# The third matrix's chains in a fused Winograd MLP: differences, roundings and products moved against each other

## The chip, the cores and the metric

The kernel runs on one core of a Trainium2 chip. The metric is device time in microseconds (us) of one launch. TensorE (PE in the profile) multiplies, VectorE (DVE) and ScalarE (ACT) work between the products, GpSimd (POOL) takes differences and sums from SBUF, and SyncE (SP) issues nearly all the DMAs. Each engine runs its own instructions strictly in order.

## The reference

For x of 2 x 3008 x 256, two filters of 1505 x 256 and the weights of two MLPs:

```
y  = irfft(rfft(x, axis=1) * (filt_r + 1j*filt_i))      # then 6016 x 256
h  = y @ w_in;  z = (h * sigmoid(h)) @ w_out             # w_in 256 x 2048, w_out 2048 x 256
g  = z @ w_gate; v = z @ w_val                           # 256 x 1536 each
out = (g * sigmoid(g) * v) @ w_out2                      # 1536 x 256
```

All inputs and outputs are float32. TensorE multiplies rounded values (fp32r), so each operand is split into a rounded high part (a cast on ScalarE) and a rest (a subtraction on VectorE), and each product is three matmuls.

## The kernel before, in words

The transform and the first MLP fill the first half. The change lies in the second MLP, which runs from about 585 us to the end.

**Pairs.** The 6016 tokens are cut into six blocks of up to 1024, and the 1536 hidden columns into six parts. `Pair(t, u)` computes one part for one block, 36 pairs in all. Gate and value are each one 2x2 block product in Winograd's form with seven products: numbers 1, 2 and 4 take weights that stay in SBUF (`w`), numbers 3, 5, 6, 7 weights loaded per pair (`wst`, `load_s2`). A `Gate` leaves its results in PSUM banks. Their order in code is `p15`, `p6`, product 2, `p3`, `p7`, `p4`. `p7` ends with an addition on VectorE (line 885) that reads the bank that `p4` then adds to, so the first matmul of `p4` waits for it; ScalarE copies out or moves a bank at lines 852, 855 and 870. For the gate, `p4` comes after the value's `p15`, for the value after the next pair's `p15`. The pair leaves two tiles, `ga` (upper half of the products, pool `late["p"]`) and `c` (pool `mid`), in `raw[u]`.

**Chains.** The third matrix takes two pairs' tiles (p = 0, 1), so there are 18 chains, three per block, of 14 steps each: seven products in the order of `AT7 = (1, 5, 6, 2, 7, 3, 4)`, each for both p. A step's work is spread over time by `tick()`, which each pair calls seven times:

- `product7` (line 1110): three matmuls of step i, put in a queue that PE drains between the pair's matmuls, one for two of those.
- `lower7` (line 1066, VectorE): the rest `ho` of step i + AHEAD - 1.
- `high7` (line 1061, ScalarE): the rounding `ho` of step i + AHEAD, in a new tile of `mid`.
- `sum7` (line 1056, GpSimd): the difference that products 5, 6, 7 and 4 need, of step i + AHEAD + 2. In place in `ga` for 5 and 7 and in `c` for 4, in a tile `x6` for 6. Number 7 overwrites the operand of 1, number 4 that of 2, so each waits until `lower7` has read it.
- `load7` (line 1074, SyncE): the weights `w7` of two products (512 KB), issued eight steps ahead, in a tile of `mid`.

When a product is complete, `after7` copies or adds it (lines 1082 to 1097), and GpSimd adds at line 1104.

**Order.** It is written out by hand: the program order of each engine is that of the code, `clock` says how far the chain is behind the pairs (it starts at -16 and goes up by one per tick), and `later(u, k, ...)` hangs loads, splits of the next block's operands (`xo`, lines 784 and 787), differences (`xr`, line 767) and the output (`store2`, VectorE transposes and DMAs) on the k-th place in pair u. After the last pair the remaining ticks run by themselves.

**Tiles.** `mid` has 33 tiles of 4 KB per partition, one kind for all names (`ho`, `w7`, `wst`, `c`, `x6`, `x2`, `xr`, `xo`, `oa`, `ob` and nine tiles of weights that stay). In the second MLP `late["p"]` is a pool `last` of nine tiles of the same size, which only `ga` uses. A new tile waits for the last reader of the tile whose place it takes.

Of the kernel before, what the change touches and what calls it, by code (L numbers as in the profile page):

```python
# [12 lines left out]
F32R = mybir.dt.float32r  # L13
U32 = mybir.dt.uint32
AF = mybir.ActivationFunctionType
ALU = mybir.AluOpType
# [13 lines left out]
P = 128  # L30
# [89 lines left out]
def fft_filter_mlp_kernel(  # L120
# [13 lines left out]
    nc = tc.nc  # L134
# [47 lines left out]
    def mid(shape, name, dtype=F32):  # L182
        return mp.tile(shape, dtype, tag="mid", name=name)
# [237 lines left out]
    wt, late = {}, {}  # L421
# [328 lines left out]
    def size2(t):  # L750
        return min(STEP2, NTOK - STEP2 * t)
# [204 lines left out]
    class Pair:  # L956
# [27 lines left out]
        def run(self, old, side):  # L984
# [5 lines left out]
            if old:  # L990
                old.tail()
            side(-1)
            tick()
            g.p6()
            if old:
                old.join()
            side(0)
            tick()
            g.add(g.a, 2, last=True)
            a = late["p"].tile([P, STEP2], F32, tag="mid", name="ga")  # L1000
# [3 lines left out]
            g.p3()  # L1004
            nc.scalar.activation(a[:, n:m], g.b, AF.Silu)
            tick()
            g.p7()
            side(1)
# [22 lines left out]
            self.join()  # L1031

    raw, x6, ops7, w7, low7, done7 = {}, {}, {}, {}, {}, {}
    AHEAD = 3
    clock = [-16]

    def where(i):
        c, r = divmod(i, 14)
        return c, AT7[r // 2], r % 2

    def view(c, k, p):
        u = 2 * c + p
        n = size2(u // 6) // 2
        a, b = raw[u]
        if k == 6:
            return x6[c][:, p, :n]
        v, l = {1: (a, 0), 5: (a, 1), 7: (a, 0), 2: (b, 0), 4: (b, 0), 3: (b, 1)}[k]
        return v[:, n * l:n * l + n]

    def sum7(c, k, p):  # L1050

        if k == 6 and p == 0:
            x6[c] = mid([P, 2, 512], "x6")
        if k in (5, 6, 7, 4):
            a, b = {5: (5, 1), 6: (3, 5), 7: (6, 1), 4: (2, 6)}[k]
            nc.gpsimd.tensor_tensor(view(c, k, p), view(c, a, p), view(c, b, p), op=ALU.subtract)  # L1056

    def high7(c, k, p):
        x = ops7[c, k, p] = mid([P, 2, 512], "ho", F32R)
        v = view(c, k, p)  # L1060
        nc.scalar.copy(x[:, 0, :v.shape[-1]], v)  # L1061

    def lower7(c, k, p):
        x, v = ops7[c, k, p], view(c, k, p)
        n = v.shape[-1]
        nc.vector.tensor_tensor(x[:, 1, :n], v, x[:, 0, :n], op=ALU.subtract)  # L1066
        if k == 4:
            del raw[2 * c + p]

    def load7(c, r):  # L1070
        q = c % 3
        w = mid([P, 2, 512], "w7", F32R)
        n = min(2, 7 - 2 * r)
        nc.sync.dma_start(w[:, :n].bitcast(F32), d7[q][:, 2 * r:2 * r + n])
        for i in range(n):
            w7[c, AT7[2 * r + i]] = w[:, i].rearrange("p (j l c) -> p j l c", j=2, l=2)
# [41 lines left out]
    CHAINS = 3 * NBLK2  # L1118

    def tick():  # L1120
        i = clock[0]
        clock[0] += 1
        inside = lambda i: 0 <= i < 14 * CHAINS
        if inside(i):
            queue.extend((product7, *where(i), k) for k in range(3))
        if inside(i + AHEAD - 1):
            lower7(*where(i + AHEAD - 1))
        if inside(i + AHEAD):
            high7(*where(i + AHEAD))
        if inside(i + AHEAD + 2):  # L1130
            sum7(*where(i + AHEAD + 2))
        if inside(i + 8):
            c, r = divmod(i + 8, 14)
            if r % 4 == 0:
                load7(c, r // 4)
# [78 lines left out]
    for b in range(len(WIDE)):  # L1214
        i = len(units) + 32 * b
# [10 lines left out]
    for q in range(4):  # L1226
        i = (22, 42, 60, 67)[q]
# [24 lines left out]
    later = lambda u, k, fn, *args: todo2.setdefault((u, k), []).append((fn, args))  # L1252
# [7 lines left out]
    later(0, 0, split_x2, 0, 4)  # L1260
    for t in range(1, NBLK2):
        for m in range(2):
            later(6 * t + 2 + m, 1, store2, t - 1, m)
        u = 6 * t - 6
        later(u + 2, 0, load_x2, t)
        later(u + 3, 1, prep_x2, t, 0)
        later(u + 3, 3, prep_x2, t, 1)
        for k, n in ((0, 1), (1, 5), (3, 6)):
            later(u + 4, k, split_x2, t, n)

        for k, n in ((3, 2), (4, 3), (4, 7)):
            later(u + 5, k, split_x2, t, n)
        later(u + 6, 0, split_x2, t, 4)
# [6 lines left out]
    for k in range(FILL_X, 8):  # L1280
        i = 8 + 5 * k // 2
# [6 lines left out]
    for h in range(12):  # L1288
        q, i = h // 2, 31 + 5 * h // 2
# [258 lines left out]
```

## Time and profile before

| | us |
|---|---|
| median of three runs | 1222.85 |
| lowest, highest | 1219.66, 1224.13 |
| profiled execution, its own time | 1225.84 |
| its span, first to last instruction | 1224.1 |
| PE busy | 1137.0 |
| DVE busy | 898.8 |
| ACT busy | 787.8 |
| POOL busy | 557.8 |

Busy time is the union of an engine's instructions in the profiled execution. Between the span and the execution's own time lie 1.7 us. In timelines a row gives start, duration, engine, line, operation and tiles; what stands in brackets is how long the engine had been idle before and what ended that.

### The profile page before, as it was taken

The page shows a single profiled execution, that of the slowest core. Times are in us where ns is not written, and L with a number is a line of the kernel's source. Part 1 is how long each engine was busy: PE and PEld are TensorE (multiplying, and loading weights), DVE is VectorE, ACT ScalarE, POOL GpSimd, SP SyncE. Part 2 cuts the span into 40 slices and gives each one's busy share as a digit, 9 for nine tenths or more (in the row PEclk, how much of TensorE's full clock was granted, in tenths as well). Part 3 has the DMA queues.
Part 4 walks back from the last instruction along what each step waited for, and adds up shares of the span by engine and source line. Part 5 has one row for each costly group of instructions (what it writes and reads, how often), then busy time and mean ns, then how long its engine had stood idle before and what let it go on. Part 6 is the DMA issues. An engine that isn't in the chain of part 4 may idle for free.

```text
span 1224.1 us, 15232 instructions
## 1 busy us (share of the span) xinstructions
PE 1137.0 (93%) x4993; PEld 921.4 (75%) x4993; DVE 898.8 (73%) x1262; ACT 787.8 (64%) x1482; POOL 557.8 (46%) x423
## 2 busy tenths in 40 slices
PE   9999999999999999999997898889789879978985
PEld 7588888988888888888775676677567657757873
DVE  5977455665766867866486887779688787958986
ACT  5798666676777776855665566566556655656662
POOL 3658545633424536231063455346354544625444
PEclk9999999999999999999999999999999999999997
DMA  9964442364544554454443353445245334534531
GB/s 253 293 194 122 144 153 87 121 211 146 169 152 156 197 190 155 155 198 154 158 169 103 129 163 122 129 131 163 95 126 161 110 129 145 144 111 135 142 121 30
DMA packets 130110, 182.45 MB, mean 149 GB/s; under 512 B 56816, under 2 KB 84336, under 8 KB 130032
## 3 DMA queue, kind: packets, MB, share of 16 engines
q1 hardware_dynamic: 129584, 181.29, 46.7%
q8 instruction: 39, 0.64, 0.2%
q14 instruction: 39, 0.32, 0.1%
q10 hardware_dynamic: 448, 0.20, 0.1%
HBM read 138.99 MB, written 42.47 MB: 148 GB/s over the span
## 4 chain that ended last, share of the span: by engine, by line
PE 69%; DVE 16%; ACT 5%; issue 5%; DMA 3%; POOL 2%; DVEq 0%; SPq 0%; ACTq 0%; POOLq 0%
PE bk L818 16%; PE acc L731 14%; PE bk L1110 7%; DVE ho L1066 6%; PE acc L708 6%; PE h L658 6%; PE y L818 5%; PE xa L818 4%; PE xb L818 4%; DMA w<-d 2%; PE s L209 2%; DVE c L885 2%; PE s L397 2%; DVE bk L879 2%; PE s L206 1%
## 5 line engine op out<-in xcount | busy, mean ns | idle before, releaser
L818 PE MATMUL bk<-xo,wst 128*128 128x512 f32 (+1 forms) x864 | 290.1, 397 | 21.4 <-ACT u L870 13.2
L1110 PE MATMUL bk<-ho,w 128*128 128x512 f32 (+1 forms) x756 | 288.2, 399 | 3.5 <-DVE ho L1066 3.5
L731 PE MATMUL acc<-h,w 128*128 128x512 f32 x768 | 283.6, 389 | 0.0
L818 PE MATMUL bk<-xo,w 128*128 128x512 f32 (+1 forms) x648 | 218.9, 403 | 48.8 <-DVE c L885 48.5
L818 PEld LDWEIGHTS bk<-xo,wst 128*128 128x128 f32 x864 | 164.3, 192 | 65.3 <-ACT u L870 19.6
L818 PEld LDWEIGHTS bk<-xo,w 128*128 128x128 f32 x648 | 124.3, 194 | 87.9 <-DVE c L885 46.0
L1110 PEld LDWEIGHTS bk<-ho,w 128*128 128x128 f32 x756 | 147.4, 196 | 33.4 <-DVE ho L1066 6.7
L731 PEld LDWEIGHTS acc<-h,w 128*128 128x128 f32 x768 | 144.2, 188 | 29.7
L1066 DVE TENSOR_TENSOR ho<-ga,ho 128x512 fp32r<-128x512 f32 (+1 forms) x108 | 118.0, 1094 | 12.4 <-ACT ho L1061 12.4
L1056 POOL TENSOR_TENSOR c<-c,x 128x512 f32<-128x512 f32 (+1 forms) x36 | 57.5, 1611 | 146.8 <-DVE ho L1066 136.8
L1061 ACT CAST ho<-ga 128x512 fp32r<-128x512 f32 (+1 forms) x108 | 66.2, 613 | 45.8 <-POOL c L1056 28.4
L708 PE MATMUL acc<-h,w 128*128 128x512 f32 (+1 forms) x384 | 95.4, 376 | 0.0
L1104 POOL TENSOR_TENSOR oa<-oa,s 128x512 f32<-128x512 f32 (+1 forms) x24 | 34.8, 1452 | 131.0 <-DVE s L1082 131.0
L1066 DVE TENSOR_TENSOR ho<-c,ho 128x512 fp32r<-128x512 f32 (+1 forms) x108 | 92.5, 876 | 0.0
L1056 POOL TENSOR_TENSOR ga<-ga 128x512 f32<-128x512 f32 (+1 forms) x36 | 57.0, 1586 | 62.3 <-DVE ga L1022 62.3
L658 PE MATMUL h<-xh,w 128*128 128x512 f32 (+1 forms) x248 | 83.6, 379 | 0.1
L708 PEld LDWEIGHTS acc<-h,w 128*128 128x128 f32 x384 | 71.2, 188 | 11.2
L666 DVE TENSOR_TENSOR h<-h,h 128x512 fp32r<-128x512 f32 (+1 forms) x64 | 41.4, 655 | 47.8 <-ACT h L665 46.4
L818 PE MATMUL xa<-xo,w 128*128 128x512 f32 x192 | 75.3, 394 | 0.0
L818 PE MATMUL y<-xo,wst 128*128 128x512 f32 x192 | 74.7, 389 | 0.0
L1061 ACT CAST ho<-c 128x512 fp32r<-128x512 f32 (+1 forms) x108 | 65.3, 614 | 14.3 <-PE bk L818 5.1
L818 PE MATMUL xb<-xo,wst 128*128 128x512 f32 x192 | 74.5, 390 | 0.0
(153 smaller groups left out, 2345.5 us busy)
## 6 DMA issues: line engine op xcount, KB each, us to landing
w<-d SPq DMA_DIRECT2D x54, 512.0 KB, 3.6
wst<-ds_g SPq DMA_DIRECT2D x36, 512.0 KB, 4.1
wst<-ds_v SPq DMA_DIRECT2D x36, 512.0 KB, 3.4
wst<-ds SPq DMA_DIRECT2D x32, 512.0 KB, 4.8
zt<-d SPq DMA_DIRECT2D x16, 384.0 KB, 4.7
d<-z SPq DMA_DIRECT2D x11, 512.0 KB, 4.4
d<-x SPq DMA_DIRECT2D x22, 256.0 KB, 2.3
d<-wst SPq DMA_DIRECT2D x21, 256.0 KB, 2.2
```

The lines of the kernel that those rows point to most:

```text
L209: nc.tensor.matmul(o, csp[:k, mp_, r:r + n], x[xp_], start=(i == 0), stop=(i == 2))
L397: nc.tensor.matmul(ps[:, col:col + n], zt_of[c // 2, g][:, 3 * (c % 2) + t, :], c4[:, o:o + n], start=(t == 0), stop=(t == 2), skip_group_ ...
L658: nc.tensor.matmul(ps[:, :n], wt[key, f // 4, g][:, wpart, o:o + P], x[xpart][:, g, :n], start=(g == 0 and k == 0), stop=(g == 1 and k == 2),)
L666: nc.vector.tensor_tensor(h[:, 1, :n], u[:, :n], h[:, 0, :n], op=ALU.subtract)
L708: nc.tensor.matmul(a[:, :n], w[:, wpart, o:o + 128], h[:, xpart, :n], start=(f == 0 and k == 0), stop=(f == 15 and k == 2),)
L731: nc.tensor.matmul(a, w[:, wpart, o:o + 128], h[xpart][:, n * l:n * l + n], start=(f == 0 and k == 0), stop=(end and k == 1), skip_group_c ...
L818: nc.tensor.matmul(o, w(wpart), x[:, xpart, :o.shape[-1]], start=(first and k == 0), stop=(last and k == 2), skip_group_check=True,)
L1056: nc.gpsimd.tensor_tensor(view(c, k, p), view(c, a, p), view(c, b, p), op=ALU.subtract)
L1061: nc.scalar.copy(x[:, 0, :v.shape[-1]], v)
L1066: nc.vector.tensor_tensor(x[:, 1, :n], v, x[:, 0, :n], op=ALU.subtract)
L1104: nc.gpsimd.tensor_tensor(o, o, s, op=ALU.add)
L1110: nc.tensor.matmul(o, w7[c, k][:, p, wpart], ops7[c, k, p][:, xpart, :n], start=(k in (1, 5) and p == 0 and i == 0), stop=(k in (2, 3, 4) ...
```

## The change

```diff
-    AHEAD = 3
-    clock = [-16]
+    AHEAD = 4
+    clock = [-20]
+    SUMS = {-7: (5, 0), -6: (5, 1), -4: (6, 0), -3: (6, 1), 1: (7, 0), 2: (7, 1), 5: (4, 0), 6: (4, 1)}
...
         if k == 6 and p == 0:
             x6[c] = mid([P, 2, 512], "x6")
-        if k in (5, 6, 7, 4):
-            a, b = {5: (5, 1), 6: (3, 5), 7: (6, 1), 4: (2, 6)}[k]
-            nc.gpsimd.tensor_tensor(view(c, k, p), view(c, a, p), view(c, b, p), op=ALU.subtract)
+        a, b = {5: (5, 1), 6: (3, 5), 7: (6, 1), 4: (2, 6)}[k]
+        nc.gpsimd.tensor_tensor(view(c, k, p), view(c, a, p), view(c, b, p), op=ALU.subtract)
...
-        w = mid([P, 2, 512], "w7", F32R)
+        w = late["p"].tile([P, 2, 512], F32R, tag="mid", name="w7")
...
-        if inside(i + AHEAD + 2):
-            sum7(*where(i + AHEAD + 2))
+        for o in (0, 14):
+            c, r = divmod(i + o, 14)
+            if 0 <= c < CHAINS and r - o in SUMS:
+                sum7(c, *SUMS[r - o])
...
-            later(6 * t + 2 + m, 1, store2, t - 1, m)
+            later(6 * t + 3 + m, 1, store2, t - 1, m)
```

The chain's products come four ticks later against the pairs. Roundings are four steps ahead of their product, rests three. The eight differences of a chain, before at steps -3, -2, -1, 0, 3, 4, 7 and 8 of that chain, are at steps -7, -6, -4, -3, 1, 2, 5 and 6. `w7` takes its tiles from `last`, which `ga` uses, and no longer from `mid`. `store2` is called one pair later.

## Rows read from the trace of the kernel before

**Rows 1.** The waits of PE, 585 to 1213 us: total, times, longest (us).
```profile
PE bk L818 <- DVE c L885: 48.5, 33, 3.4
PE bk L818 <- ACT u L870: 13.2, 15, 1.6
PE bk L818 <- ACT bk L852: 7.8, 8, 1.2
```
**Rows 2.** Busy time by stretch: PE, PEld, DVE, ACT, POOL (instructions), clock, DMA.
```profile
822.84:928.74 105.90, 92.50 (x379) 72.26 (x379) 84.38 (x112) 63.87 (x121) 49.79 (x32) 0.97 0.44 132
865.65:869.05 3.40, 3.40 (x10) 2.63 (x11) 0.00 (x0) 1.72 (x4) 0.00 (x0) 0.57 0.00 0
906.60:910.00 3.40, 3.40 (x10) 2.65 (x9) 1.30 (x2) 2.27 (x5) 0.22 (x1) 0.56 0.29 82
1193.50:1213.00 19.50, 15.37 (x52) 10.98 (x50) 18.82 (x24) 6.70 (x14) 12.19 (x9) 0.84 0.00 0
585.00:1193.50 608.50, 538.34 (x2249) 428.27 (x2248) 477.16 (x638) 371.31 (x709) 274.14 (x179) 0.97 0.44 135
```
**Rows 3.** Timeline of PE: two matmuls of a stretch without gaps.
```profile
917.59 0.39 PE L1110 MATMUL bk<-ho,w 128*128 128x512 f32 x1
...
918.27 0.39 PE L1110 MATMUL bk<-ho,w 128*128 128x512 f32 x1
```
**Rows 4.** Timeline of PE: gaps of the block that begins at 822.84 us.
```profile
822.84 0.96 PE L818 MATMUL bk<-xo,w 128*128 128x512 f32 x3 [0.56 <-DVE c L885]
...
850.29 0.50 PE L818 MATMUL bk<-xo,wst 128*128 128x512 f32 x1 [0.62 <-ACT u L870]
...
865.37 1.22 PE L818 MATMUL bk<-xo,wst 128*128 128x512 f32 x2 [1.25 <-ACT bk L852]
...
876.21 0.98 PE L818 MATMUL bk<-xo,w 128*128 128x512 f32 x3 [2.29 <-DVE c L885]
...
882.17 0.74 PE L818 MATMUL bk<-xo,wst 128*128 128x512 f32 x2 [1.54 <-ACT u L870]
...
904.74 0.47 PE L818 MATMUL bk<-xo,w 128*128 128x512 f32 x1 [3.41 <-DVE c L885]
```
**Rows 5.** Timeline of POOL and ACT and DVE, 859 to 881 us.
```profile
859.76 3.42 POOL L1056 TENSOR_TENSOR ga<-x,ga 128x512 f32<-128x512 f32 x2
...
869.29 0.62 ACT L1061 CAST ho<-x 128x512 fp32r<-128x512 f32 x1 [1.92 <-PE bk L1110]
...
871.68 0.62 ACT L784 CAST xo<-xr 128x512 fp32r<-128x512 f32 x1 [1.28 <-PE bk L818]
...
872.33 0.69 DVE L787 TENSOR_TENSOR xo<-xr,xo 128x512 fp32r<-128x512 f32 x1 [6.77 <-ACT xo L784]
...
877.56 2.93 POOL L1056 TENSOR_TENSOR c<-c,x 128x512 f32<-128x512 f32 x2 [14.39 <-DVE ho L1066]
...
880.52 0.62 ACT L1061 CAST ho<-ga 128x512 fp32r<-128x512 f32 x1 [5.70 <-POOL c L1056]
```
**Rows 6.** Timeline of POOL and DVE, 898 to 919 us.
```profile
898.81 1.74 POOL L1056 TENSOR_TENSOR ga<-ga 128x512 f32<-128x512 f32 x1
899.32 1.77 DVE L1066 TENSOR_TENSOR ho<-ga,ho 128x512 fp32r<-128x512 f32 x1
...
902.22 1.78 DVE L1066 TENSOR_TENSOR ho<-ga,ho 128x512 fp32r<-128x512 f32 x1
...
903.41 3.41 POOL L1056 TENSOR_TENSOR ga<-x,ga 128x512 f32<-128x512 f32 x2
903.92 0.68 DVE L885 TENSOR_TENSOR c<-bk,s 128x512 f32<-128x512 f32 x1
...
918.47 0.68 DVE L1066 TENSOR_TENSOR ho<-ga,ho 128x512 fp32r<-128x512 f32 x1
```
**Rows 7.** The waits of SP's queue, 600 to 1224 us: total, times, longest (us).
```profile
SPq L1074 <- PE bk L1110: 166.2, 39, 9.8
SPq L637 <- PE bk L1110: 108.2, 37, 4.3
```

## The prediction

> **What bounds the kernel now.** I read the waits of PE first, then busy time by stretch, then the gaps of PE one by one in one block of the second MLP, and last what ACT, DVE and POOL did before each gap. Six pairs make a block, and a block repeats. From 822.84 to 928.74 us it takes 105.90 us and PE runs 379 matmuls [rows 2]; by count they are 6 x 63 = 378, a pair's own 42 and 21 of the chains. In a stretch without gaps three matmuls take 918.27 - 917.59 = 0.68 us, 0.227 each [rows 3]. 378 x 0.227 = 85.8 us, so 20.1 us of a block are lost. Eleven gaps of over 0.3 us sum to 13.3. Two stretches of 3.4 us at a granted clock of 0.57 and 0.56 [rows 2], nearly all of them at 1.2 GHz, come right behind gaps (865.37, 904.74 [rows 4]) and cost half their length, 1.7 us each. The other 3.4 us are slower starts behind gaps. The whole stretch of pairs is 608.5 us [rows 2], or 5.75 blocks.
>
> The gaps are of two kinds. Five (0.56, 0.47, 1.09, 1.25, 3.41, sum 6.78; first and last in [rows 4]) are waits for line 885 on a DVE that is late because its subtractions collide with POOL. The rest of a chain's operand (line 1066) takes 0.68 us alone and 1.77 or 1.78 beside a difference on POOL; line 885, which reads PSUM, keeps its 0.68 beside one [rows 6]. I call these collisions. Before the last gap POOL runs (5,1), both 6 and both 7 without a break, 898.81 to 906.82 [rows 6].
>
> The other six (0.62, 0.52, 1.25, 0.33, 2.29, 1.54, sum 6.55; four of them in [rows 4]) begin on ACT. Its cast of x at 869.29 waited 1.92 us for PE line 1110, though the value was ready when POOL began the next difference at 859.76 [rows 5]: what it waited for was a tile of `mid`, held by an earlier matmul. The split at 871.68 waited 1.28 for the same kind of thing, DVE stood 6.77 us behind that split [rows 5], its line 885 came late and PE lost 2.29 [rows 4]. Then ACT's cast of a 7 stood 5.70 us until the second difference of 4 was done, long after its own difference had ended (859.76 + 3.42 = 863.18) [rows 5]: again a tile, and PE lost 1.54. SP says the same of `mid`: loads of `w7` waited 166.2 us for PE, `wst` 108.2 [rows 7]. `mid` is full at nearly every point. So tiles and collisions, not one busy engine, hold PE: 48.5 us show as line 885 and 13.2 + 7.8 as copies of ACT [rows 1].
>
> **The change part by part.** One step of a chain is a tick, 105.90 / 42 = 2.52 us [rows 2].
>
> *w7 out of `mid`.* Three tiles per chain live 12 steps (8 ahead, 4 of products) and the last 10: 46 steps in 14, 3.3 tiles. What the other edits add to `mid`: `ho` one step longer, 14 steps in 14, 1.0; `c` from p = 0 lives 23 steps for 20, from p = 1 17 for 14, 6 in 14, 0.4; `x6` 10 for 9, 0.1. Net 1.8 of 33 tiles become spare. The six gaps above need releases that come 0.3 to 2.3 us earlier. `mid` hands out some 13 tiles per pair of 105.90 / 6 = 17.65 us (seven `ho`, two `c`, two `wst`, a part of the others), so 1.8 tiles are 1.8 x 17.65 / 13 = 2.4 us. I take five of the six as gone and one of 1.25 as left: 5.3 us per block. Bounds: all of 6.55, or nothing if the choice of the free tile still takes a fresh one.
>
> *Differences earlier.* The instructions are the same eight per chain, 24 per block. Before, each cast came two steps after its difference; now there are three to five steps, 7 to 12 us. This removes what true waits of ACT on POOL there are; they are within the six gaps, so it earns nothing twice. On POOL's queue they stand between the additions of line 1104, which wait for products: the order becomes (5,0), (5,1), addition, both 6, addition, both 7, both 4, so no run longer than about three replaces the run of five. Collisions per difference stay as likely as they are; only their bunching falls. DVE has 84.38 busy of 105.90 [rows 2], so a delay of one collision, 1.1 us (1.78 - 0.68 [rows 6]), is mostly absorbed by the 18 matmuls (18 x 0.227 = 4.1 us) between `p7` and `p4`, and three in a row are not. Bounds for the five gaps: all 6.78 stay, or half go; I take a quarter, 1.7, nearer to the row where a single collision costs PE 0.56.
>
> *Clock.* One of the two slow stretches stands behind a gap of ACT (1.25 at 865.37 [rows 4]) that goes, the other behind the collision of 3.41 that only shrinks. One goes: 1.7 us. Bounds none and 3.4.
>
> *Chain later, rests and roundings one step earlier.* ACT and DVE do the same work, PE the same matmuls. The cast of product 1 for p = 1 stood one step behind the tick in which its `ga` is made, now four. What was hidden by pairs and now isn't is the end: 12 matmuls of 448 columns leave the stretch of pairs and run behind the last pair. There DVE is busy 18.82 of 19.50 us, so DVE sets the pace [rows 2]. Three more rests at 0.68 to 1.78 and two more additions at about 0.6 make 3.2 to 6.5 us; the pairs give back 12 x 0.227 = 2.7 at most, and some of the differences finish before that stretch. I put +1 us, between -1 and +4.
>
> *`store2` a pair later.* Same transposes and DMAs; the last ones, which nothing follows, don't move. Its two `oa` are held 40 steps for 37 or as long as before, nothing that matters.
>
> *`w7` in `last`.* `ga` lives 23 and 17 steps, 40 in 14, 2.9 tiles; with 3.3 that is 6.1 of nine, and eight at the peak (step 4: four `ga`, four `w7`). SP's queue has `wst` and `x2` behind each `w7` load; with a spare tile they go earlier, not later. Cost 0 in the forecast; the other end is a rival below.
>
> Sum per block: 5.3 + 1.7 + 1.7 = 8.7 us. I don't take all of it: a faster PE brings DVE from 84.4 / 105.9 = 0.80 to 84.4 / 97.2 = 0.87 busy, in strict order, and new gaps must come. I take a third off, 5.8. Times 5.75 it is 33 us, less 1 at the end: 1225.8 - 32 = 1194 for the profiled execution. The median of before lies 3.0 us under that execution, so 1191.
>
> **The rivals.**
>
> *Only tiles help (A).* Collisions keep their number and move: both 7, which ran in the gate's half of the even pair, now come in its value half, and both 4 in the gate's half of the odd pair. Then 5.3, less a third, is 3.5 per block: 20 us, 1225.8 - 20 + 1 - 3 = 1204. For it: a rest beside POOL takes 1.78 wherever it stands [rows 6]. Against it: four of the five gaps come from runs, not single differences. The Trainium skill (SBUF — State Buffer, "Who interferes with whom") says that a VectorE instruction with two SBUF inputs and a GpSimd one that reads SBUF exclude each other for a whole instruction, the second waiting for the first. By that rule spreading differences lowers no sum of delays, and the time would be the 1204 of this rival; the rows agree on the size of one delay, but don't show what spacing does.
>
> *DVE gives it all back (B).* DVE's 84.4 us per block are already near PE's 85.8, so PE finds it late whatever is freed: 1223. Against it: DVE idles 21.5 us per block, 6.77 of it at one place because of a tile [rows 5].
>
> *Nine tiles are too few (C), slower.* If PE falls over four steps behind the ticks, an old `w7` is still unread when a new `ga` is wanted; nine are live, and ACT's silu, ahead of the copies that PE needs, waits. Price: one such wait of 1.92 (as at 869.29 [rows 5]) per chain, 18 x 1.92 = 35 us, against the 20 of A: 1223 + 15 = 1238. It decides from nine live tiles on; by count there are eight at most, so it needs the lag or an unlucky choice of the place.
>
> **How the numbers follow.** Forecast 0.52, A 0.22, B 0.12, C 0.14. About 0.5% (6 us) is what a measurement tells from no change. Faster by more: forecast 0.52, A 0.20, B 0.02, together 0.74. Within: A 0.02, B 0.08, C 0.01: 0.11. Slower: B 0.02, C 0.13: 0.15. The range: at the low end all of 6.55, 1.7 and 1.7 with nothing given back, 10 per block, 57 us, and a little of the second slow stretch: 1164. At the high end it takes in B and the beginning of C: 1228. Forecast alone: 1175 to 1205.
>
> **What would show it.** Tiles right: SP's 166.2 us for `w7` on PE fall under 60, ACT no longer waits for POOL's differences of 4, DVE's 6.77 us behind the split is gone, and the gaps at copies of ACT (21.0 us in all [rows 1]) fall under 8. Collisions right: waits for line 885 fall from 48.5 to about 25 to 30, none over 2.5 us, while rests beside POOL still take 1.78. Half-speed stretches: one per block. Forecast wrong: `ga`'s silu waiting for a tile, or gaps at line 885 of the old sum at new places, or POOL's run as long as before because the additions don't divide it.

## The result, and the profile after

The changed kernel takes 1182.82 us (median of three runs, 1182.42 to 1185.03), the kernel before 1222.85: a ratio of 0.9676, interval 0.9648 to 0.9703, 40.0 us less. The profiled execution takes 1185.03 us with a span of 1183.2, against 1225.84 and 1224.1.

The first view is busy time by stretch, with the columns of [rows 2]: one block, the half-speed stretch behind its largest gap, and the end behind the last pair.

```profile
819.99:919.06 99.07, 91.07 (x378) 72.03 (x378) 83.58 (x112) 64.01 (x121) 47.43 (x32) 0.97 0.46 141
...
846.25:853.08 6.83, 6.20 (x15) 4.32 (x15) 3.92 (x6) 4.34 (x8) 2.56 (x2) 0.50 0.69 135
...
1149.50:1172.00 22.50, 18.87 (x66) 13.72 (x66) 21.97 (x28) 8.10 (x17) 14.40 (x11) 0.85 0.01 4
```

A block takes 99.07 us for 105.90 with the same 378 matmuls by count. From 585 us on the pairs take 564.5 us for 608.5, 44.0 less: 6.83 us times 5.75 blocks are 39.3 of it, and up to 2.7 are the matmuls of the chains that now run behind the last pair. The end holds 14 more matmuls in these windows (12 by count) and takes 22.5 us for 19.5. So the span is 40.9 us shorter. PE's waits of the second MLP answer to [rows 1]:

```profile
PE bk L818 <- DVE c L885: 31.1, 31, 3.2
PE bk L818 <- ACT bk L852: 5.3, 6, 2.1
PE bk L1110 <- DVE ho L1066: 2.2, 4, 0.6
PE bk L818 <- ACT u L870: 1.8, 2, 1.7
```

Gaps that begin at a copy of ACT fell from 21.0 to 7.1 us in all, those at line 885 from 48.5 to 31.1. In PE's timeline the block shows seven gaps of over 0.2 us for eleven [rows 4]:

```profile
845.27 0.50 PE L818 MATMUL bk<-xo,w 128*128 128x512 f32 x1 [3.21 <-DVE c L885]
847.62 1.22 PE L818 MATMUL bk<-xo,wst 128*128 128x512 f32 x2 [0.64 <-ACT bk L852]
871.23 0.96 PE L818 MATMUL bk<-xo,w 128*128 128x512 f32 x3 [0.25 <-DVE c L885]
880.54 0.47 PE L818 MATMUL bk<-xo,w 128*128 128x512 f32 x1 [1.99 <-DVE c L885]
888.80 0.96 PE L818 MATMUL bk<-xo,w 128*128 128x512 f32 x3 [0.74 <-DVE c L885]
910.77 0.50 PE L818 MATMUL bk<-xo,w 128*128 128x512 f32 x1 [0.36 <-DVE c L885]
919.06 0.98 PE L818 MATMUL bk<-xo,w 128*128 128x512 f32 x3 [0.74 <-DVE c L885]
```

They sum to 7.93 us for 13.33. Of the six gaps that were put down to tiles one is left, 0.64 for 6.55. The gaps at line 885, which the prediction put down to collisions, have not shrunk: 7.29 for 6.78. The largest of them is again a DVE that reaches line 885 late, as in [rows 6], here behind a split (787) and a rest (1066) that both stood beside differences of 6. In this view of ACT, DVE and POOL the split takes 1.82 us and the rest 1.77:

```profile
838.66 0.62 ACT L784 CAST xo<-x 128x512 fp32r<-128x512 f32 x1 [1.20 <-DVE c L982]
839.29 2.98 POOL L1056 TENSOR_TENSOR x<-c,ga 128x512 f32<-128x512 f32 x2 [2.46 <-ACT xo L784]
...
839.31 1.82 DVE L787 TENSOR_TENSOR xo<-x,xo 128x512 fp32r<-128x512 f32 x1 [0.73 <-ACT xo L784]
...
841.05 1.77 DVE L1066 TENSOR_TENSOR ho<-c,ho 128x512 fp32r<-128x512 f32 x1
...
844.54 0.68 DVE L885 TENSOR_TENSOR c<-bk,s 128x512 f32<-128x512 f32 x1
```

Not all of the 3.21 us is collision. The split's cast on ACT stood 1.20 us for line 982, whose result it doesn't read, which is how a wait for a tile looks; DVE idled 0.73 us behind that cast, and POOL's differences of 6, which don't read its result either, were let go by the same cast. By this reading a wait for a tile set the two side by side.

SP's queue answers to [rows 7]: loads of `w7` hardly wait for a tile any more, `wst`, which stayed in the large pool, waits longer.

```profile
SPq L637 <- PE bk L1110: 190.3, 33, 7.9
...
SPq L1074 <- PE bk L1110: 6.1, 1, 6.1
```

### The profile page after: what moved, and what is told of

Read it like the earlier page. It is cut to its first block, busy times and chain, and to the rows that moved or that the text cites. A ratio compares the mean times of both kernels' runs of the same rounds, so it can differ in the third digit from the quotient of the medians.

```text
span 1183.2 us, 15182 instructions
## 1 busy us (share of the span) xinstructions
PE 1127.6 (95%) x4993; PEld 919.2 (78%) x4993; DVE 887.5 (75%) x1262; ACT 788.0 (67%) x1482; POOL 544.9 (46%) x423
## 4 chain that ended last, share of the span: by engine, by line
PE 73%; DVE 17%; issue 4%; ACT 3%; DMA 1%; POOL 0%; DVEq 0%; ACTq 0%; SPq 0%; POOLq 0%
PE bk L818 16%; PE acc L731 15%; PE bk L1110 8%; PE acc L708 7%; PE h L658 7%; DVE ho L1066 6%; PE y L818 6%; PE xa L818 4%; PE xb L818 4%; DVE bk L879 2%; PE s L397 2%; DVE c L885 2%; PE s L209 2%; PE s L206 2%; DVE ga L1019 1%
## 5 line engine op out<-in xcount | busy, mean ns | idle before, releaser
L818 PE MATMUL bk<-xo,wst 128*128 128x512 f32 (+1 forms) x864 | 284.9, 393 | 5.0 <-ACT bk L852 3.1
L818 PE MATMUL bk<-xo,w 128*128 128x512 f32 (+1 forms) x648 | 216.0, 398 | 33.6 <-DVE c L885 31.1
L818 PEld LDWEIGHTS bk<-xo,w 128*128 128x128 f32 x648 | 121.7, 191 | 72.5 <-DVE c L885 37.7
L1066 DVE TENSOR_TENSOR ho<-ga,ho 128x512 fp32r<-128x512 f32 (+1 forms) x108 | 105.6, 980 | 0.6 <-ACT ho L1061 0.6
L1056 POOL TENSOR_TENSOR c<-c,x 128x512 f32<-128x512 f32 (+1 forms) x36 | 52.6, 1463 | 113.9 <-DVE ho L1066 113.9
L1066 DVE TENSOR_TENSOR ho<-c,ho 128x512 fp32r<-128x512 f32 (+1 forms) x108 | 102.3, 953 | 0.2 <-issue 0.2
L1056 POOL TENSOR_TENSOR ga<-ga 128x512 f32<-128x512 f32 (+1 forms) x36 | 47.8, 1331 | 88.4 <-DVE ga L1022 76.7
L708 PEld LDWEIGHTS acc<-h,w 128*128 128x128 f32 x384 | 71.2, 188 | 11.2
L852 ACT COPY bk<-bk 128x512 f32<-128x512 f32 (+1 forms) x72 | 41.3, 573 | 45.1 <-PE bk L818 45.0
L1056 POOL TENSOR_TENSOR ga<-x,ga 128x512 f32<-128x512 f32 (+1 forms) x36 | 50.1, 1407 | 33.5 <-DVE ho L1066 29.7
```

The lines of the kernel that those rows point to most:

```text
L708: nc.tensor.matmul(a[:, :n], w[:, wpart, o:o + 128], h[:, xpart, :n], start=(f == 0 and k == 0), stop=(f == 15 and k == 2),)
L818: nc.tensor.matmul(o, w(wpart), x[:, xpart, :o.shape[-1]], start=(first and k == 0), stop=(last and k == 2), skip_group_check=True,)
L852: nc.scalar.copy(self.y, self.a)
```

## The experiments

All times are medians of three or more runs beside runs of the kernel before on the same chip (medians of before 1221.1 to 1223.8). "Spare" is the count of tiles that the large pool has free against before, by steps held as in the prediction: +3.3 for `w7`, -1.0 for roundings four ahead, -0.4 to -0.6 for the later chain's `c`, -0.1 for a longer `x6`. The later chain always comes with `store2` a pair later. The count is a mean and doesn't rank the kernels: -0.6 takes 1231.10 us and -0.2 takes 1248.80, and the kernel with the most spare tiles is not the fastest.

| kernel | spare | us | ratio to before (interval) |
|---|---|---|---|
| before | 0 | 1222.9 | 1 |
| `w7` alone | +3.3 | 1192.67 | 0.9742 (0.9717 to 0.9767) |
| later chain alone | -0.6 | 1231.10 | 1.0081 (1.0054 to 1.0107) |
| `w7`, later chain | +2.7 | 1169.18 | 0.9563 (0.9532 to 0.9593) |
| the same, 32 tiles | +1.7 | 1179.13 | 0.9655 (0.9632 to 0.9678) |
| `w7`, later, roundings four ahead | +1.9 | 1178.84 | 0.9632 (0.9603 to 0.9661) |
| the same and differences spread: the change | +1.8 | 1182.82 | 0.9676 (0.9648 to 0.9703) |
| the change, 31 tiles | -0.2 | 1248.80 | 1.0207 (1.0181 to 1.0232) |
| the change, roundings three ahead | +2.6 | 1169.50 | 0.9576 (0.9549 to 0.9603) |

**The `w7` alone.**

```diff
-        w = mid([P, 2, 512], "w7", F32R)
+        w = late["p"].tile([P, 2, 512], F32R, tag="mid", name="w7")
```

> The kernel before with one edit: the weights w7 take their tiles from the pool of nine instead of the pool of 33; differences, roundings, products and store2 stand where they were. Theory T (tiles): the gaps of PE that begin on ACT come from tiles of the large pool, and 3.3 tiles become spare, so nearly all of those gaps go: a block takes 100 to 102 us for 105.9, and the whole 1190 to 1203 us; waits for line 885 stay at 45 to 55 us. Rival S (spacing): what helped is that the differences stand earlier and apart; then this kernel gains little, 1212 to 1223 us. Rival C (nine tiles too few): 1225 us or more.

It took 1192.67 us, 31 us less than before, as theory T had it. Its waits of PE:

```profile
PE bk L818 <- DVE c L885: 45.3, 32, 3.4
PE bk L1110 <- DVE ho L1066: 3.1, 6, 0.6
PE bk L818 <- ACT u L870: 1.6, 1, 1.6
```

21.0 us of gaps at copies of ACT [rows 1] are down to 1.6, and line 885 keeps 45.3 of its 48.5. The order of the work was not touched: one pool had too few tiles.

**The change with 31 tiles.**

```diff
-    mp = pool("mp", 33)
+    mp = pool("mp", 31)
```

> The changed kernel with 31 tiles in the large pool for 33, which takes the 1.8 spare tiles by count away again; the order of all instructions is unchanged. Theory T: the gaps that begin on ACT come back, 1205 to 1225 us (a part of it may fall in the first half, to be read by stretch). Rival S: the order sets the time, so 1180 to 1190 us.

It took 1248.80 us, 66 more than the change and beyond the expectation. At most 1.4 us of it lie before the second MLP, whose first copy at line 852 starts at 587.2 us for 585.8. PE's waits, and below them one cast of ACT with the idle time before it:

```profile
PE bk L818 <- ACT bk L852: 44.2, 20, 7.7
PE bk L818 <- DVE c L885: 35.2, 35, 2.3
```

```profile
875.12 0.62 ACT L1061 CAST ho<-ga 128x512 fp32r<-128x512 f32 x1 [4.54 <-DMA out_dram<-ob]
```

Line 885 costs 35.2 us for 31.1 in the change, while 44.2 us for 5.3 now begin at ACT's line 852; with them the granted clock of the pairs falls from 0.98 to 0.95. The cast reads `ga` and writes `ho`; it has nothing to do with the output, and yet it waits 4.54 us for an output DMA. The only tie between them is the tile: `ho` gets the place of an `ob` that is still being stored. That is how such a wait is told from a true one.

**Differences near again.** `SUMS` is no longer used, each difference stands two steps ahead of its rounding (`sum7` gets its test for products 5, 6, 7 and 4 back, not shown):

```diff
-        for o in (0, 14):
-            c, r = divmod(i + o, 14)
-            if 0 <= c < CHAINS and r - o in SUMS:
-                sum7(c, *SUMS[r - o])
+        if inside(i + AHEAD + 2):
+            sum7(*where(i + AHEAD + 2))
```

> The changed kernel with one part undone: each difference stands two steps ahead of its rounding again, in one run of four and two pairs, and no longer three to five steps ahead and spread; the chain is still four steps later, roundings four ahead, w7 in the pool of nine. Theory T: spacing is worth little, 1180 to 1192 us. Rival S: the spread is worth most of the 40 us, so 1205 to 1222 us here.

It took 1178.84 us, 4 us less than with the spread. So in the change the spread earned no time, against the prediction's 1.7 us per block. Rival S falls. PE's waits are nearly the same in all, 39.4 us here at line 885 and copies of ACT (34.4, 3.1 and 1.9) for 38.2 in the change; the granted clock of the pairs is 0.99 for 0.98.

**No differences.** The change without the 144 differences of the chains:

```diff
-            if 0 <= c < CHAINS and r - o in SUMS:
-                sum7(c, *SUMS[r - o])
...
-        if k == 6:
-            return x6[c][:, p, :n]
-        v, l = {1: (a, 0), 5: (a, 1), 7: (a, 0), 2: (b, 0), 4: (b, 0), 3: (b, 1)}[k]
+        v, l = {1: (a, 0), 5: (a, 1), 7: (a, 0), 2: (b, 0), 4: (b, 0), 3: (b, 1), 6: (b, 1)}[k]
```

> The changed kernel without the 144 differences of the chains on GpSimd (products 5, 6, 7 and 4 of the third matrix get operands that lack them, so that part of the output is left out); everything else stands as in the changed kernel. It prices the collisions of VectorE with these differences and any wait for them. Theory T with collisions: the waits for line 885 (31 us) fall under 8, rests at line 1066 take 0.68 us, the half-speed stretches in the pairs go, and the time is 1140 to 1155 us. Rival (VectorE is simply full, collisions are hidden): 1172 to 1183 us.

It took 1138.98 us, just under the expected 1140. PE's first wait, and one of its gaps:

```profile
PE bk L818 <- DVE c L885: 11.2, 15, 1.5
```

```profile
767.83 0.47 PE L818 MATMUL bk<-xo,w 128*128 128x512 f32 x1 [1.40 <-DVE c L885]
```

and the rests (line number 1064 here), in the view by line:

```profile
L1064 DVE TENSOR_TENSOR ho<-c,ho 128x512 fp32r<-128x512 f32 (+1 forms) x144 | 105.9, 741 | 0.3
L1064 DVE TENSOR_TENSOR ho<-ga,ho 128x512 fp32r<-128x512 f32 (+1 forms) x108 | 78.4, 728 | 0.6 <-ACT ho L1059 0.6
```

A rest takes 0.73 to 0.74 us on the mean, and waits at line 885 fall from 31.1 to 11.2, a little above the 8 expected. Without the differences the kernel is 1182.8 - 1139.0 = 44 us faster. That holds collisions and half-speed, but also what else goes with the differences: the casts' waits for them, and the tile of `x6`, which is held 10 of 14 steps and of which this kernel has no need. The run doesn't divide the 44. The gap of 1.40 stands where the change has 1.99 (880.54): so 1.4 of that one is a full DVE queue and no collision with a difference of the chains. Three such gaps, 2.3 us per block (1.40, 0.42, 0.49), stay of the change's 7.29.

**The later chain with `w7` moved**, roundings three ahead:

```diff
-    clock = [-16]
+    clock = [-20]
...
-            later(6 * t + 2 + m, 1, store2, t - 1, m)
+            later(6 * t + 3 + m, 1, store2, t - 1, m)
```

> The kernel with w7 alone moved (1192.7 us) plus the chain four steps later and store2 a pair later; roundings still three steps ahead, rests two, differences two steps ahead of the roundings. The kernel with differences near (1178.8 us) has all this and roundings four ahead. Theory L (the later chain gives the 14 us, since products find operands and results of the pair older): 1178 to 1184 us. Rival R (rounding and rest one step earlier give it): 1188 to 1194 us.

It took 1169.18 us, better than either theory had it, and 9.7 better than the version with roundings four ahead. So the later chain, with `store2` a pair later, gives 23.5 us over `w7` alone, as theory L had it in kind; its reason (older operands and results) is not shown. Rival R has the wrong sign here. A block:

```profile
750.25:844.50 94.25, 88.25 (x379) 70.18 (x379) 82.66 (x112) 63.65 (x120) 47.90 (x33) 1.00 0.48 148
```

94.25 us at full clock; DVE is busy 82.66 of them, 0.88, more than the 0.87 at which the prediction wanted to give a third back. Its first wait of PE, and then the same group of rests in the two kernels, `w7` alone first:

```profile
PE bk L818 <- DVE c L885: 27.3, 30, 1.6
```

```profile
L1066 DVE TENSOR_TENSOR ho<-ga,ho 128x512 fp32r<-128x512 f32 (+1 forms) x108 | 126.7, 1174 | 0.0
```

```profile
L1066 DVE TENSOR_TENSOR ho<-ga,ho 128x512 fp32r<-128x512 f32 (+1 forms) x108 | 106.1, 996 | 0.7 <-ACT ho L1061 0.6
```

Waits at line 885 fall by 18 us, the longest from 3.4 to 1.6 us, and the granted clock of the pairs rises from 0.97 to 1.00; the end takes 23.9 us for 18.6. Rests on `ga` fall from 1174 to 996 ns, while those on `c` rise from 857 to 921: the chain's differences now meet other work of DVE. Which of the moved meetings did it, and what `store2` has in it, was not taken apart.

**The later chain alone** is that edit on the kernel before, with `w7` in the large pool.

> The kernel before with the chain four steps later and store2 a pair later, and nothing else: w7 stays in the large pool, roundings three ahead. Together with the three kernels at 1223, 1192.7 (w7 alone) and 1169.2 (both) it tells whether the two add up. Theory T: without spare tiles the later chain, which holds c longer (0.4 tiles), gains nothing or loses, 1220 to 1250 us. Rival (lateness is worth 23 us by itself): 1195 to 1205 us.

It took 1231.10 us, 0.8% slower than before. Line 885 has improved here too (48.5 before), but ACT takes it back, 24.1 us at line 852 and 8.5 at 870 for 21.0 in all:

```profile
PE bk L818 <- DVE c L885: 36.7, 33, 3.7
PE bk L818 <- ACT bk L852: 24.1, 7, 4.6
```

What is left over lies mostly at the end: from the last matmul of the pairs to the last of the chains it takes 23.7 us for 18.3. So the two parts don't add: `w7` alone -31 us, lateness alone +8 to +10, both -54. In these four kernels lateness pays only with tiles to spare.

**32 tiles** in the version with `w7` and the later chain (`mp` from 33 to 32).

> The version at 1169.2 us with 32 tiles in the large pool for 33. Roundings four ahead hold one tile more on the mean and cost 9.7 us (1178.8 against 1169.2). Theory T (that cost is the tile): taking one tile away here costs about the same, 1175 to 1183 us. Rival (it is the order of the earlier roundings and rests): 1167 to 1172 us.

It took 1179.13 us, as theory T had it, against 1178.84 with roundings four ahead. But the waits are not the same:

```profile
PE bk L818 <- DVE c L885: 26.6, 34, 1.6
PE bk L818 <- ACT bk L852: 7.6, 9, 1.5
```

Here 26.6 us stand at line 885 and 9.5 at copies of ACT (7.6 and 1.9 at line 870), with roundings four ahead 34.4 and 5.0. So in time a rounding one step earlier costs what one tile costs, but the equal times don't show that the tile is all of it.

**The change with roundings three ahead** (`AHEAD = 4` to 3, `SUMS` kept).

> The changed kernel with roundings three steps ahead for four; differences stay spread at their steps, now four to six steps ahead of the roundings. Against the version at 1169.2 us it differs in the place of the differences alone. If the spread costs what it cost with roundings four ahead (1182.8 against 1178.8): 1171 to 1176 us. If spread differences help once a tile is free: under 1167 us.

It took 1169.50 us, 13 less than the change, and the same as the version with near differences (1169.18). With a tile more the spread costs nothing and gains nothing in time. The 1171 to 1176 expected was a little too much. The traces of the two are not the same:

```profile
PE bk L818 <- DVE c L885: 21.6, 32, 2.0
PE bk L818 <- ACT bk L852: 7.1, 8, 2.1
```

```profile
836.94 0.50 PE L818 MATMUL bk<-xo,w 128*128 128x512 f32 x1 [0.35 <-DVE c L885]
```

```profile
L1066 DVE TENSOR_TENSOR ho<-ga,ho 128x512 fp32r<-128x512 f32 (+1 forms) x108 | 92.4, 870 | 0.8 <-ACT ho L1061 0.8
```

With the spread, waits at line 885 are 21.6 us for 27.3, rests on `ga` take 870 ns for 996 and those on `c` 856 for 921, and between 770 and 960 us DVE is busy 158 us for 167. Waits at copies of ACT are 8.9 us (7.1, and 1.8 at line 870) for 3.5 (1.6 and 1.9). So the spread does shorten DVE's delays, and about as much is lost at ACT; what ACT waits for there was not tested. The gap of 0.35 stands where the change has its 3.21, without the cast that waited for a tile.

**`store2` and the second differences of x**, both on the version with roundings four ahead and near differences (1178.84):

```diff
-            later(6 * t + 3 + m, 1, store2, t - 1, m)
+            later(6 * t + 2 + m, (4, 2)[m], store2, t - 1, m)
```

> The kernel with differences near (1178.8 us), with store2 of the first half of the columns one place earlier (behind the seventh tick of the third pair of a block) and of the second half at the third place of the fourth pair, so that its two transposes (1.29 us) no longer stand in the fifth pair with the splits of x. Theory Q (a gap at line 885 is what DVE's queue holds before it, 2.63 us per block there): the gap of 2.6 falls to 1.3 to 1.8 and the time to 1170 to 1176 us. Rival: DVE gives it back at the place where the transposes go: 1177 to 1182 us.

1170.72 us (ratio 0.9577, 0.9540 to 0.9613), 8 less. The gap of 2.63 us before 851.64 (shown in the last section) is 1.25 here, as theory Q had it, and no half-speed stretch is left in the pairs. The place of the transposes in DVE's queue is worth that much; `oa` is also given back sooner, which was not tested by itself. On top of it:

```diff
-        later(u + 3, 3, prep_x2, t, 1)
+        later(u + 5, 0, prep_x2, t, 1)
```

> As the kernel with store2 earlier, and in addition the second pair of differences of x (line 767) two pairs later, so that GpSimd has no run of eight differences. Collisions by run (theory Q): the gaps of the fourth pair of a block (0.72, 0.42, 1.17) fall by 1 us or so in all, 3 to 6 us under the kernel with store2 earlier. Rival (collisions only move, as the spread of the chain's differences showed): within 3 us of it, or slower since the second pair of differences now meets the splits.

1164.58 us (0.9526, 0.9495 to 0.9556), the fastest of all, 6 us under the last. Since the later differences also hold a tile of `xr` shorter, this run doesn't tell collisions from tiles.

> The fastest plain version so far (w7 moved, chain later, roundings three ahead, differences near: 1169.2 us) with the two edits that took the kernel with roundings four ahead from 1178.8 to 1164.6 us: store2 earlier and the second differences of x two pairs later. If the two gains add up as they stand (14 us): 1155 us; if the gap of 2.6 that they mended is already smaller here (1.59 per block): 1158 to 1165 us.

Both edits on the version at 1169.18 gave 1168.50 us (0.9565, 0.9542 to 0.9588): nothing. The expectation missed; waits at line 885 are 26.7 us for 27.3. This kernel differs from the fastest (1164.58) only in its roundings, three ahead for four, and is 4 us slower by the medians. So the step of lead that cost 9.7 and 13 us above costs nothing here. Both edits also give tiles back sooner (`oa`, `xr`); that this is why fits, but no run shows it.

**Eight tiles in the small pool** (`pool("last", 9` to 8) on the version at 1178.84.

> The kernel with differences near (1178.8 us) with eight tiles for nine in the pool of ga and w7. By count of the program eight tiles are live at the peak, so nine leave one spare. Theory T (a pool without a spare tile makes its users wait): 1185 to 1230 us, with waits of SP at line 1074 or of ACT's silu at line 1001. Rival: eight are enough because the loads stand eight steps ahead: 1177 to 1181 us.

1180.13 us (0.9655, 0.9621 to 0.9689): no change. Eight are enough, and rival C of the prediction is rejected.

## Why the prediction was right, and where not

It forecast 1191 and a range of 1164 to 1228; the time is 1182.82. The forecast was 32 us, measured are 40. Of its signs, copies of ACT under 8 us (7.1) and SP's wait for `w7` under 60 came true; line 885 stayed at 31.1 with a longest of 3.2, over the 25 to 30 and 2.5, and the one half-speed stretch of the block is twice as long. Step by step, per block:

- **Tiles, 5.3 us: right, and shown.** 5.9 of 6.55 went (0.64 left). `w7` alone gives 31 us, and 31 tiles take more than all of it away. The waits that named matmuls were waits for tiles.
- **Spread of the differences, 1.7 us: wrong in the time.** The gaps at line 885 sum to 7.29 for 6.78, and near differences are as fast or 4 us faster. Nor are these gaps collisions alone, as the prediction took them: in the change 0.73 us stand behind a tile, and 2.3 stay without the chains' differences. Rival A, that collisions only move, fits the change. With a tile more it doesn't: there the spread takes 5.7 us off line 885 and 126 ns off a rest on `ga`, and ACT's waits take it back. The Trainium skill (SBUF — State Buffer, "Who interferes with whom") says which instructions exclude each other, and rests at 0.68 or 1.77 us agree; what the prediction drew from it, that spreading lowers no sum of delays, these traces don't bear out.
- **Clock, 1.7 us: wrong.** Two stretches of 3.4 us at half speed [rows 2] became one of 6.8 behind the gap of 3.21; the cost per block is the same.
- **A third given back, 2.9 us: wrong.** DVE went from 0.80 to 83.58 / 99.07 = 0.84 busy, and the gaps as a whole fell from 13.33 to 7.93; the later version runs at 0.88. Slower starts behind gaps even gave 1.5 us: 99.07 - 85.8 - 7.93 - 3.4 = 1.9 for 3.4.
- So 5.9 - 0.5 + 0 + 1.5 = 6.9, the 6.83 measured, against 8.7 - 2.9 = 5.8 predicted. The two terms that failed (3.4) and the discount that wasn't due (2.9) nearly cancel.
- **Later chain and earlier roundings, priced at nothing but the end: wrong twice.** With tiles to spare the later chain, with `store2` a pair later, is worth 23.5 us; the roundings cost 9.7, and 13 in the change itself. The end came out as put: 22.5 for 19.5 us, of which the pairs give back up to 2.7.
- **`store2` at nothing: not so in another version.** Its place is worth 8 us in the version with near differences; in the change itself it was not run.
- **Nine tiles too few: rejected.** SP's waits at line 1074 for PE fell from 166.2 to 6.1 us, under the 60 named as the sign.

By the runs the 40 us are `w7` -31, the later chain -23.5, earlier roundings +9.7 and the spread +4. The prediction's mechanism, one pool without room, is right and carries most of it. That 1191 came so near is luck in part: terms that failed and a discount that wasn't due offset each other, and of the later chain's 23.5 us, priced at nothing, about 14 were lost again by two other parts of the change.

What stays open is why the later chain meets fewer collisions (the times of its rests show that it does, not which place did it), and why a step of lead costs 10 us in one version and nothing in another.

## What to carry to other kernels

When an engine in strict order waits for something its instruction doesn't use (a cast for an old matmul, or for an output DMA), look at the pool its result comes from; moving one kind of tile to a pool with room was worth 31 us here, and one tile 10. Work that runs further ahead holds tiles longer, so first count what each step of lead holds, and test lead and room apart, and again when something else has changed: each alone misled here. Don't judge a spread of one engine's operations by the time alone: here it shortened a neighbour's delays and lost as much elsewhere. And a gap that ends at a late engine is not all collision; take the suspect out and see what stays.

## What was not expected of the hardware

Gaps of the same size at the same place were followed by half speed in one block and not in the next. In the version with near differences at 1178.84 us, PE waited 2.63 us for line 885 twice, one block apart:

```profile
851.64 0.96 PE L818 MATMUL bk<-xo,w 128*128 128x512 f32 x3 [2.63 <-DVE c L885]
...
949.41 0.96 PE L818 MATMUL bk<-xo,w 128*128 128x512 f32 x3 [2.63 <-DVE c L885]
```

```profile
852.77:856.18 3.41, 3.41 (x10) 2.63 (x9) 1.87 (x4) 1.18 (x3) 0.00 (x0) 0.50 0.01 2
...
949.41:955.00 5.59, 5.58 (x24) 4.54 (x25) 4.50 (x8) 3.16 (x7) 0.00 (x0) 1.00 0.03 7
```

Behind the first the granted clock is 0.50 (1.2 GHz) for 3.4 us, behind the second it stays at 1.00. In the kernel before, too, 1.25 us (865.37) are followed by half speed and 2.29 (876.21) are not [rows 4]: from 868.60 to 906.15 us the clock is 1.00. In the version with the later chain 30 waits at line 885 of up to 1.6 us each leave the pairs at 1.00. So what a gap costs in clock is read from the stretch behind it, and not from its size.
